# The second half of x of pair 1, issued behind the constant table and the first mask of pair 0

## The chip, the cores and the metric

The kernel runs on one core of one Trainium2 chip. The metric is the device time of one execution in microseconds. Before the change it is 122.68 us, the median of three runs (122.57 to 123.12). The engines are named as in the profile: PE is TensorE (PEld its weight load), DVE is VectorE, ACT is ScalarE, POOL is GpSimd, SP is SyncE, which here only issues DMAs.

## The reference

A state-space attention step (Mamba-2 form) is followed by a bilinear feed-forward. Per batch and head the sequence of 768 is worked in chunks, with a decaying state carried from chunk to chunk:

```
M       = (C B^T) * L                       # L: decay between two positions, causal
y       = M x + (C state) * decay_to_i
state   = decay_full * state + sum_j B_j x_j * decay_from_j
out     = ((y Wa) * (y Wb)) Wout            # 3072 tokens, 256 -> 1536 -> 256
```

There are 4 batches, 8 heads, head size 32 and state size 16; x, B, C and the weights are float32 in memory, and the kernel computes its products in float16.

## The kernel before, in words

The 768 positions are cut into 6 blocks of 128 (the decay is arranged so that a block of 128 replaces the reference's chunks of 32). The 4 batches are taken two at a time, so that there are 12 "pairs": pair p is block p // 2 of batches 2(p % 2) and 2(p % 2) + 1. Pairs 0 and 1 are the first block of all batches.

For each pair the kernel scales B and C by decay factors (scale_bc), transposes them on PE (transposes), multiplies them into scores (scores, L458 for the first pairs), masks these with the causal table (mask, L497 on DVE or L494 and L495 on ACT and POOL), scales x to float16 (scale_x, L366 on ACT), and multiplies masked scores by x (pv, whose matmuls are L518). The result is evacuated to X2T (for pair 1 by ACT in L581) and is the moving operand of the feed-forward: matmuls with Wa and Wb (L734 in units_mm, L721 in unit_mm), a copy of the Wa part (L745, ACT), a product (L752, DVE) and the output matmuls with Wo.

The order of the work is written out by hand: the tile framework runs under a manual schedule, every engine executes its instructions in the order of the program, and tile dependencies become semaphore waits. A dependency that the data do not ask for can be added with tc.add_manual_dep. One stands here already: the first half of x of pair 1 waits for f0, the first reciprocal on DVE (L874, L875).

A pair's x is 256 KB in float32. For the first four pairs it is loaded in two halves, one for each of the two batches (load1, whose DMA is L165 for all callers). For pair 1 both halves are issued on SP's queue in L246 and L247, ahead of the constant table c32 (L248, 32 x 148 float32, read by POOL in L942 and by PE in L963). At the same time POOL issues the loads of B and C of pair 1 and then the first halves of the weights (L259 to L263): Wa in two pieces, then Wb in two pieces, with a cast to float16 on the way. The second halves of the weights follow on POOL in L897 and L898. SP's next DMA after these is the store of the decay rows, in L958.

The first work on both weights is that of pair 0: three groups of Wa matmuls for pair 0 (L915, L918, L919), with the scores and masks of pair 1 between them, and three groups of Wb matmuls (L931, L933 to L935), with pv(1), the product of pair 1's masked scores and its x, standing behind the first four of them (L932). On ACT the order there is: the copy of the first Wa group (L920), scale_x(1) in L921, the copies of the second and third group (L922), and then the evacuation of pv(1). So x of pair 1 is wanted by ACT between the first and the second copy.

The four masks of pair 0 are DVE's L889, L890, L894 and L895, each a product of 128 x 512 scores with the causal table. The first of these is the one that the change names.

Of the kernel before, what the change touches and what calls it, by code (L numbers as in the profile page):

```python
# [14 lines left out]
ALU = mybir.AluOpType  # L15
PSUM = bass.MemoryType.PSUM
AFTER = mybir.DependencyInfo(mybir.DependencyClass.Sync, mybir.DependencyReason.DATA)
# [12 lines left out]
def kernel(  # L30
# [13 lines left out]
    nc = tc.nc  # L44
# [109 lines left out]
    def by_token(t_):  # L154
        return t_.rearrange("p h r n -> p (h r n)").rearrange("p (t h n) -> p t h n", t=2, h=H)

    def load1(eng, p, which, bt, i0=0, n=64):
        blk, bp = divmod(p, NBP)
        if p >= P0:
            return eng.dma_start(  # L160
                by_token(pair_in[p][which])[:, bt],
                (B, C, x)[which][2 * bp + bt, :, blk * Q : (blk + 1) * Q, :].rearrange("h q n -> q h n"),
            )
        src = (B, C, x)[which][2 * bp + bt, :, blk * Q + 2 * i0 : blk * Q + 2 * i0 + 2 * n, :]
        return eng.dma_start(  # L165
            pair_in[p][which][64 * bt + i0 : 64 * bt + i0 + n].rearrange("i h r n -> i h (r n)"),
            src.rearrange("h (i r) n -> i h (r n)", r=2),
        )
# [57 lines left out]
    for p_ in range(3):  # L226
# [17 lines left out]
    nc.vector.memset(c32, 0.0)  # L244
    nc.vector.memset(Pq, 0.0)
    x1 = load1(nc.sync, 1, 2, 0)  # L246
    load1(nc.sync, 1, 2, 1)  # L247
    nc.sync.dma_start(c32[0:BH], p32_t.ap())  # L248
    nc.gpsimd.affine_select(
        out=ident, in_=ident, compare_op=ALU.is_equal, fill=0.0, base=0, pattern=[[-1, 128]], channel_multiplier=1  # L250
    )
    for bt in range(2):
        v = causal[64 * bt : 64 * bt + 64]
        nc.gpsimd.affine_select(  # L254
            out=v, in_=v, compare_op=ALU.is_ge, fill=0.0, base=0, pattern=[[-1, 2], [1, Q]], channel_multiplier=-2
# [46 lines left out]
    def second_factors(fps):  # L302
        F = fps[:, 0:32].rearrange("p (r c) -> p r c", r=2)
        for r in range(2):
            for bt in range(2):
                nc.tensor.matmul(
                    F[64 * bt : 64 * bt + 64, r],
                    Pr[:, 1].rearrange("p (i r) -> p r i", r=2)[:, r],
                    selr[:, bt].rearrange("p b h -> p (b h)"),
                    start=True,  # L310
                    stop=True,
                    skip_group_check=True,
                    tile_position=(0, 64 * bt),
                )
# [167 lines left out]
    def product0(m2, e):  # L482

        return (
            st[0]["T1"][:, 4 * m2 : 4 * m2 + 4].rearrange("p (m e) r q -> p e m (r q)", e=2)[:, e],
            (SC0, SC1)[m2][:, :, e * 256 : e * 256 + 256],
            causal.rearrange("p r q -> p (r q)").unsqueeze(1).broadcast_to((128, 2, 2 * Q)),
        )

    def mask(out_in, by_pool=False):  # L490
        o_, i_, c_ = out_in
        if by_pool:
            tmp = mid.tile([128, *c_.shape[1:]], f32, name="tmp", tag="tmp")
            nc.scalar.copy(tmp, i_)  # L494
            nc.gpsimd.tensor_tensor(out=o_, in0=tmp, in1=c_, op=ALU.mult)  # L495
        else:
            nc.vector.tensor_tensor(out=o_, in0=i_, in1=c_, op=ALU.mult)  # L497

    def pv_u(p, u, py, first, flip=2):
        s = st[p]  # L500
# [365 lines left out]
    def pull(p):  # L866
# [19 lines left out]
    scores(0)  # L886
    fps = bank("fps")
    second_factors(fps)
    mask(product0(0, 0))  # L889
    mask(product0(0, 1))  # L890
    scale_bc(1, 0, nc.gpsimd)
    scale_x(0, nc.scalar)
    nc.scalar.copy(f_c(1), fps[:, 0:32].rearrange("p (r b h) -> p r b h", r=2, b=NBP))
    mask(product0(1, 0))  # L894
    mask(product0(1, 1))  # L895
    scale_bc(1, 1, nc.gpsimd)
# [3 lines left out]
        out=causal_q, in_=causal_q, compare_op=ALU.is_ge, fill=0.0, base=0, pattern=[[1, Q]], channel_multiplier=-1  # L900
# [25 lines left out]
    for w in range(2):  # L926
# [16 lines left out]
        out=hsx[0:BH],  # L943
        in0=hs.unsqueeze(1).broadcast_to((BH, nb, NG)),
        in1=selb.rearrange("p (b g) -> p b g", b=nb),
        op=ALU.mult,
# [291 lines left out]
```

## Time and profile before

| | us |
|---|---|
| median of three runs | 122.68 |
| the profiled execution | 122.38 |
| its span, first to last instruction | 120.6 |
| PE busy | 116.2 (96%) |
| DVE busy | 93.0 (77%) |
| ACT busy | 75.4 (62%) |
| POOL busy | 70.3 (58%) |

The granted TensorE clock is 1.0 throughout. The profile's times are counted from the start of the span. "Busy" leaves out DMA-issuing instructions and waits. A DMA issue is shown on the queue of the engine that issues it (SPq, ACTq, POOLq), and its "landing" is counted from the start of that issue to the completion. The DMA queues are q1 (issued by SP), q10 (issued by ACT) and q0 (issued by POOL); all of them share 16 DMA engines. The chain is followed back from the last instruction to whatever released each step.

### The profile page before, as it was taken

To read this page: it belongs to the slowest core of one execution; us is meant where nothing else is said; L and a number is where in the kernel's file an instruction comes from. 1 tells how busy PE (TensorE), PEld (TensorE's weight loads), DVE (VectorE), ACT (ScalarE), POOL (GpSimd) and SP (SyncE) were. 2 spreads that over 40 slices of the span, in tenths; PEclk is the share of its full clock that TensorE was granted. 3 is DMA by queue.
4 is the path that set the end of the run, shared out by engine and by line. 5 is a ranking of instruction groups with operands and counts; after the bars stand their busy time and mean duration, and the time that the engine had idled before them with its cause. 6 is when DMAs were issued, how large, how long until landed. Compare 5 with 4: busy or idle time off the path is not lost.

```text
span 120.6 us, 3714 instructions
## 1 busy us (share of the span) xinstructions
PE 116.2 (96%) x1436; PEld 79.2 (66%) x1436; DVE 93.0 (77%) x184; ACT 75.4 (62%) x155; POOL 70.3 (58%) x96
## 2 busy tenths in 40 slices
PE   6999999999999999999999999999999999999990
PEld 2346789889898898644476464686464684555890
DVE  4999999994998979699995999767998445847100
ACT  0458867837668856987669657655866737566220
POOL 7995999999996997199998099119043000000000
PEclk9999999999999999999999999999999999999999
DMA  3999989993886593866469701012001012010122
GB/s 64 194 167 213 211 179 224 152 192 66 91 160 118 51 137 75 133 87 150 108 191 232 242 8 43 0 49 87 3 0 43 7 42 87 0 43 5 43 87 87
DMA packets 35953, 12.29 MB, mean 102 GB/s; under 512 B 29840, under 2 KB 35248, under 8 KB 35936
## 3 DMA queue, kind: packets, MB, share of 16 engines
q1 hardware_dynamic: 30976, 6.71, 27.3%
q0 software_dynamic: 2688, 4.92, 20.1%
q10 hardware_dynamic: 2272, 0.43, 1.8%
q8 instruction: 11, 0.18, 0.6%
q14 instruction: 6, 0.05, 0.2%
HBM read 11.20 MB, written 3.21 MB: 119 GB/s over the span
## 4 chain that ended last, share of the span: by engine, by line
PE 87%; DMA 5%; POOL 4%; issue 1%; ACT 0%; DVE 0%
PE ops L824 18%; PE aps L799 17%; PE bps L799 17%; PE ops L767 9%; PE aps L721 8%; PE bps L721 8%; DMA Wb<-in_moe_w_b_dram 5%; PE SC L443 2%; PE SC L503 1%; PE bps L734 1%; POOL bn L165 1%; POOL cn L165 1%; PE SC L518 1%; PE tr L409 1%; POOL causal L254 1%
## 5 line engine op out<-in xcount | busy, mean ns | idle before, releaser
L745 ACT COPY asb<-aps 128x512 f32<-128x512 f32 x71 | 41.3, 587 | 12.8 <-PE aps L799 8.8
L809 DVE TENSOR_TENSOR hkb<-bps,asb 128x512 f16<-128x512 f32 x48 | 32.1, 690 | 10.2 <-ACT asb L745 9.7
L799 PE MATMUL aps<-XB,Wa 128*128 128x512 f16 x96 | 28.6, 379 | 0.0
L799 PE MATMUL bps<-XB,Wb 128*128 128x512 f16 x96 | 28.5, 379 | 0.0
L824 PE MATMUL ops<-Wo,hkb 128*128 128x256 f16 (+1 forms) x204 | 22.6, 266 | 0.0
L824 PEld LDWEIGHTS <-hkb 128*128 128x128 f16 x204 | 18.6, 98 | 3.1
L497 DVE TENSOR_TENSOR t<-SC,causal_q 128x512 f16<-128x512 f32 x24 | 15.5, 683 | 2.4 <-PE SC L443 2.4
L799 PEld LDWEIGHTS <-Wb 128*128 128x128 f16 x96 | 9.9, 103 | 10.9
L752 DVE TENSOR_TENSOR hk<-bps,asb 128x512 f16<-128x512 f32 x24 | 15.8, 685 | 1.5 <-ACT asb L745 1.3
L495 POOL TENSOR_TENSOR t<-tmp,causal_q 128x512 f16<-128x512 f32 x8 | 9.2, 1160 | 13.0 <-ACT tmp L494 12.7
L799 PEld LDWEIGHTS <-Wa 128*128 128x128 f16 x96 | 9.7, 103 | 9.2
L836 ACT ACTIVATE osb<-ops 128x256 f32<-128x256 f32 (+1 forms) x16 | 6.1, 378 | 12.3 <-PE ops L824 12.2
L721 PE MATMUL bps<-X2T,Wb 128*128 128x256 f16 x84 | 12.4, 272 | 0.0
L368 POOL TENSOR_SCALAR x<-xn 128x512 f16<-128x512 f32 x8 | 11.9, 1489 | 0.7
L721 PE MATMUL aps<-X2T,Wa 128*128 128x256 f16 x80 | 11.9, 273 | 0.0
L767 PE MATMUL ops<-Wo,hk 128*128 128x256 f16 x96 | 11.6, 273 | 0.0
L767 PEld LDWEIGHTS <-hk 128*128 128x128 f16 x96 | 8.9, 98 | 1.3
L721 PEld LDWEIGHTS <-Wa 128*128 128x128 f16 x84 | 8.4, 104 | 0.8 <-issue 0.2
L721 PEld LDWEIGHTS <-Wb 128*128 128x128 f16 x84 | 8.6, 103 | 0.5
L497 DVE TENSOR_TENSOR t<-SC,causal 128x512 f16<-128x512 f32 x13 | 8.2, 681 | 0.4 <-PE SC L458 0.3
L494 ACT COPY tmp<-SC 128x512 f32<-128x512 f32 x11 | 6.5, 592 | 1.7 <-PE SC L458 0.6
L202 DVE STREAM_TRANSPOSE tq<-mq 128x256 f16<-128x256 f16 x10 | 7.5, 745 | 0.0
(115 smaller groups left out, 142.1 us busy)
## 6 DMA issues: line engine op xcount, KB each, us to landing
out_dram<-osb SPq DMA_DIRECT2D x18, 128.0 KB, 2.1
xn<-in_x_dram POOLq DMA_DIRECT2D x6, 256.0 KB, 5.2
rq<-in_C_dram SPq DMA_DIRECT2D x32, 32.0 KB, 3.0
Wo<-in_moe_w_out_dram POOLq DMA_DIRECT2D x2, 384.0 KB, 5.8
bn<-in_B_dram SPq DMA_DIRECT2D x6, 128.0 KB, 4.6
out_dram<-osb SPq DMA_DIRECT2D x11, 64.0 KB, 1.5
xn<-in_x_dram SPq DMA_DIRECT2D x4, 128.0 KB, 5.2
xn<-in_x_dram SPq DMA_DIRECT2D x2, 256.0 KB, 5.3
```

Source lines behind the costliest of these rows:

```text
L202: nc.vector.transpose(t_.rearrange("p t (i g) -> p g t i", g=4), st[("scaled", blk, which)][:, :, 2 * bp : 2 * bp + 2].rearrange("p g t e ...
L368: eng.tensor_scalar(xo, xi, XS, None, ALU.mult)
L494: nc.scalar.copy(tmp, i_)
L495: nc.gpsimd.tensor_tensor(out=o_, in0=tmp, in1=c_, op=ALU.mult)
L497: nc.vector.tensor_tensor(out=o_, in0=i_, in1=c_, op=ALU.mult)
L721: nc.tensor.matmul(ps[:, kk * 2 * Q : (kk + 1) * 2 * Q], w_up(W, k, f), X2T[:, p, :, f], start=(f == 0), stop=(f == 1), skip_group_check=True,
L745: (nc.vector.tensor_copy if on_dve else nc.scalar.copy)(asb, a_ps)
L752: nc.vector.tensor_tensor(out=s["hk"][:, 2 * k2 : 2 * k2 + 2, :].rearrange("p k q -> p (k q)"), in0=b_ps, in1=asb, op=ALU.mult)
L767: nc.tensor.matmul(o_ps[:, 0:d_model], hk[:, k, bt * Q : (bt + 1) * Q], Wo[:, k, :], start=(k == 0), stop=(k == NK - 1), skip_group_check= ...
L799: nc.tensor.matmul(t_, w_up(W, k, f), XB[:, blk - P0 // NBP, f].rearrange("p t j q -> p (t j q)"), start=(f == 0), stop=(f == 1), skip_gro ...
L809: return lambda: nc.vector.tensor_tensor(out=s["hk"][:, k], in0=ps[1], in1=asb, op=ALU.mult)
L824: nc.tensor.matmul(o_ps[:, 0:w], hk[:, k, c * Q : (c + 1) * Q], Wo[:, k, cs], start=(k == 0), stop=(k == NK - 1), skip_group_check=True,)
```

## The change

The second half of x of pair 1 is issued behind the constant table on SP's queue. It also gets a manual dependency on the first mask of pair 0, so that SP waits for that DVE instruction before it issues the load. For this, mask() returns the DVE instruction.

```diff
     x1 = load1(nc.sync, 1, 2, 0)
-    load1(nc.sync, 1, 2, 1)
     nc.sync.dma_start(c32[0:BH], p32_t.ap())
+    x1b = load1(nc.sync, 1, 2, 1)
...
         else:
-            nc.vector.tensor_tensor(out=o_, in0=i_, in1=c_, op=ALU.mult)
+            return nc.vector.tensor_tensor(out=o_, in0=i_, in1=c_, op=ALU.mult)
...
     scores(0)
     fps = bank("fps")
     second_factors(fps)
-    mask(product0(0, 0))
+    m0 = mask(product0(0, 0))
+    tc.add_manual_dep(x1b.ins, m0.ins.name, AFTER, reason="weights ahead of the second half of pair 1's x")
     mask(product0(0, 1))
```

## The prediction

> **What bounds the kernel now.** I read the chain that ended last first, over the first 15 us, where the moved load and everything it feeds lie (columns: start, length in us, what).
>
> ```profile
> 6.23 6.09 DMA Wb<-in_moe_w_b_dram
> 12.32 0.05 issue
> 12.37 0.62 PE bps L734 x4
> 12.99 0.40 PE SC L518 x32
> 13.39 0.99 PE bps L734 x8
> ```
>
> The chain runs through a weight transfer, Wb, up to 12.37, and from there on TensorE (PE) alone. The reader is to see two things: the weight is what PE waited for here, and 0.6 us later PE does the L518 matmuls, which multiply by x of pair 1. So I asked next how much idle time PE has, before and after this place (windows of time; the columns are the stretch, its length, busy us of PE, PEld, DVE, ACT, POOL, the granted clock, the DMA share and GB/s).
>
> ```profile
> 5.70:14.40 8.70, 8.07 (x177) 5.06 (x177) 8.14 (x21) 6.38 (x17) 7.23 (x13) 1.00 1.13 199
> 14.40:117.90 103.50, 103.41 (x1250) 72.69 (x1249) 80.94 (x148) 67.50 (x138) 58.22 (x72) 1.00 0.45 93
> ```
>
> From 14.4 to 117.9 PE is idle for 103.50 - 103.41 = 0.09 us. Work that PE starts late at 14.4 therefore ends late by the same amount: there is nothing behind it that could take a delay up. Between 5.7 and 14.4 it is idle for 8.70 - 8.07 = 0.63 us. That is all that better-timed loads could win here.
>
> Third, the timeline of ScalarE (ACT) at that place. It shows who makes the x that L518 needs.
>
> ```profile
> 11.76 0.58 ACT L745 COPY asb<-aps 128x512 f32<-128x512 f32 x1
> 12.24 0.63 ACT L366 ACTIVATE x<-xn 128x512 f16<-128x512 f32 x1
> 12.78 1.06 ACT L745 COPY asb<-aps 128x512 f32<-128x512 f32 x2
> 13.72 0.62 ACT L581 ACTIVATE X2T<-SC 128x512 f16<-128x512 f32 x1
> ```
>
> ACT has no gap from 11.76 to 14.34. The scaling of x of pair 1 (L366) starts at 12.24 because the copy ahead of it is done, with no wait on a load listed. Behind it in order stand two copies and the evacuation into X2T, whose end at 14.34 releases PE's L721 matmuls at 14.39. A late L366 thus delays L518 and, through ACT's order, L721 by the same time.
>
> Fourth, when the halves of x arrive: the tile xn between 5 and 14 us.
>
> ```profile
> L165 SPq DMA_DIRECT2D xn<-in_x_dram x2: 601/618/636, 5.2 to 5.9; - x2
> DMA to landing us min/median/max: 5.1/5.6/6.0
> ```
>
> The first half, issued at 5.2, takes 5.1 us (lands 10.3); the second, issued at 5.9, takes 6.0 (lands 11.9). ACT needs it at 12.24, so the half that is moved has 0.35 us to spare.
>
> **The change, part by part.**
>
> The handle that mask() now returns issues no instruction: 0.
>
> The constant table takes the second half's place on SyncE's queue, at 5.9 instead of 6.54, and its 0.62 us issue then ends at 6.5. It took 5.6 us and landed at 12.1; its first reader is POOL at 16.97 (L942). Earlier is worth 0, and even 4.8 us later would cost nothing. On SP's queue the load waits now, and behind it stands only the store of rows at 17.82, which waits 10.6 us for DVE; a load issued by 8.8 is 9 us clear of it. POOL's queue is not touched: 0.
>
> The wait on the first mask is the main part. DVE runs four masks from 7.43, in order:
>
> ```profile
> 4.94 0.25 DVE L874 RECIPROCAL fB<-fC 128x16 f32<-128x16 f32 x1
> 7.43 2.48 DVE L497 TENSOR_TENSOR t<-SC,causal 128x512 f16<-128x512 f32 x4
> ```
>
> One takes 0.68 (median by line), so the first ends at 8.11. The first half hangs in the same way on L874, which ends at 5.19, and is issued at 5.2, so a release costs some 0.03 to 0.05. The second half is issued at 8.15, that is 2.25 us later than now. With 0.35 to spare this is late by 1.9 us if it still takes 6.0, and harmless if it takes 4.1 or less. On DVE the extra signal can cost at most some 0.02 (one semaphore event of that line is 21 ns), which the 2.48 us row of masks absorbs or passes on once; I take 0.
>
> How long does it take from 8.15? The bounds: 4.2 us, the one 128 KB half that ACT's queue issued at 2.9, before any weight was asked for, and 6.0, the moved half itself, which now queues right behind the first half. The four x loads of this size on SP took 5.1, 6.0, 5.3 and 5.1. I take 5.1, the first half of the same x: same size and queue, weights moving beside it, and no other half right ahead, which is what the moved half will meet. Packets by window bear this out (queue, packets, MB, share of 16 engines; the three fences are 7 to 8 us, 8 to 9 us and 11 to 12 us):
>
> ```profile
> q0 software_dynamic: 83, 0.12, 89.4%
> q1 hardware_dynamic: 11, 0.00, 1.9%
> ```
>
> ```profile
> q0 software_dynamic: 85, 0.11, 63.6%
> q1 hardware_dynamic: 465, 0.12, 53.9%
> ```
>
> ```profile
> q0 software_dynamic: 140, 0.19, 107.6%
> q1 hardware_dynamic: 33, 0.01, 9.3%
> ```
>
> SP's queue (q1) moves almost nothing from 7 to 8 though the first half's issue ended at 5.85: its bytes start some 2.1 us after that, and last from 8.0 to 10.3, its landing. The weights (q0) keep the engines as busy at 11 as at 7, so a half issued at 8.15 to 8.77 starts at about 10.9 and lands at 10.9 + 2.3 = 13.2, which agrees with 8.15 + 5.1 = 13.25.
>
> The sum: L366 starts 0.04 after landing (pair 0's last piece landed at 7.39 and its L366 began at 7.43), at 13.29 instead of 12.24: +1.05 us. All that follows on ACT and PE shifts by that. With the bounds, 4.2 gives 12.39, so +0.15; 6.0 gives 14.19, so +1.95.
>
> Against it stands what the weights gain. The moved half's bytes ran mostly between 9 and 11 us; q1 held 54, 38 and 36% of the engines from 8 to 11, some 1.3 us for both halves, so 0.6 for one. Wb, then without that company, can land up to 0.6 us earlier, and PE's 0.21 us wait before 12.37 goes. It is worth nothing: the four L734 matmuls finish 0.21 earlier and PE then stands before L518, waiting for L366. That wait is late next, with x undelayed until 12.87, with the change until 13.92. I book 0, with 0.2 as its bound.
>
> The profiled execution took 122.38 (span 120.6 and 1.8 around it), 0.30 under the median of 122.68. 122.38 + 1.05 = 123.43 on its own scale, 123.73 on the median's. I predict 123.7.
>
> **The rivals.**
>
> Hidden (not slower). The half starts moving soon after its issue and lands before 12.2, so nobody waits. For it: the very first load on this queue, issued from 0.80 to 1.20, moves its first packets before 2.0, at most 0.8 us after the issue. With that start the half would begin at 8.77 + 0.8 = 9.6 and land at 9.6 + 2.3 = 11.9, and the time would be 122.7, at best 122.5 with the 0.2 of Wb. Against it: that load met idle engines, the first half met weights and needed 2.1. It decides at a flight of 4.1 us; up to 4.65 the loss stays under 0.6. The Trainium skill (DMA: Bandwidth & Descriptors, Specifications) gives about 0.6 us to the first byte on this path, which speaks for this rival: by it the landing would be some 11.7 and the sum 0; the trace agrees for the first load and not for the first half of x. Chance 0.23, counting every loss below 0.6.
>
> Later still. The half shares the engines with four more weight transfers (two of 192 KB under way, two of 384 KB issued at 8.63 and 9.38) and again takes 6.0: +1.95, 124.6. For it: q0's share is above 100% from 11 us on. Against it: three of four such loads took 5.1 to 5.3. Chance 0.14, for anything over 5.8 us.
>
> Faster. Wb lands early, x lands in time as well, and all of PE's 0.63 us of idle time before 14.4 goes: 122.05. That idle time has other owners (only 0.21 is put down to Wb). Chance 0.03.
>
> **How the numbers follow.** The forecast, a flight of 4.65 to 5.8 us, has 0.60 and its own range of 123.3 to 124.4. About 0.5%, 0.6 us, is what a measurement of this kernel can tell from no change. Slower is forecast plus later still, 0.74; within it 0.23; faster 0.03. The range of 122.6 to 124.6 leaves out the faster case (0.03), some 0.07 of the hidden one and 0.09 of the late one.
>
> **What would show it.** In the changed kernel's profile: the second half's issue at 8.1 to 8.2, with the table's before it at 5.9; a flight near 5.1 us; ACT idle between the first L745 copy (ending 12.34) and L366 for about 1 us, released by the load of xn; PE idle about 1 us before L518, with the first four L734 starting at 12.2; L721 at about 15.4; Wb no longer in the chain, xn in its place. It is wrong if L366 still starts at 12.24 (the hidden case), if the flight is far from 5.1, or if PE's stall does not show at the end, which would mean idle time behind 14.4 that the windows do not show.

## The result, and the profile after

The changed kernel takes 124.36 us in the median of six executions, against 122.75 of the kernel before beside it: 1.6 us slower, a ratio of 1.014 (95% interval 1.010 to 1.018). A second measurement of the same kernel gave 1.009 (1.006 to 1.012). In some executions of the kernels that stall here the granted clock is 0.973 to 0.987 and the time one to some five us longer; the medians keep these, the ratios leave them out where they are over 1.5% above the fastest, and one of 125.47 us stays in the 1.014, which would be 1.012 without it.

The profiled execution took 124.28, with a span of 122.6 instead of 120.6. The chain that ended last, from 7 to 18 us (start, length in us, what):

```profile
7.40 0.72 DVE t L497 x2
8.12 5.97 DMA xn<-in_x_dram
...
14.71 1.05 ACT asb L745 x2
15.77 0.51 ACT X2T L581
16.27 0.04 issue
16.32 0.60 PE aps L721 x4
```

It now runs through the first mask, then through the moved half of x in place of Wb, and then through ACT's order, up to the L721 matmuls. These start at 16.32 instead of 14.39, 1.93 us later, and the span grew by 2.0. ACT's timeline at that place (start, length, what; in brackets the idle time before it and what ended it):

```profile
11.87 0.58 ACT L745 COPY asb<-aps 128x512 f32<-128x512 f32 x1 [0.22 <-PE aps L734]
14.18 0.63 ACT L366 ACTIVATE x<-xn 128x512 f16<-128x512 f32 x1 [1.73 <-DMA xn<-in_x_dram]
14.71 1.05 ACT L745 COPY asb<-aps 128x512 f32<-128x512 f32 x2
15.65 0.61 ACT L581 ACTIVATE X2T<-SC 128x512 f16<-128x512 f32 x1
```

ACT waits 1.73 us for the load before L366, and everything behind keeps its distance: 14.18 to 15.65 is 1.47, and was 12.24 to 13.72. PE's timeline:

```profile
12.70 0.62 PE L734 MATMUL bps<-X2T,Wb 128*128 128x256 f16 x4 [0.43 <-DMA Wb<-in_moe_w_b_dram]
14.86 0.42 PE L518 MATMUL SC<-t,x 64*32 64x128 f16 x32 [1.54 <-ACT x L366]
15.21 1.05 PE L734 MATMUL bps<-X2T,Wb 128*128 128x256 f16 x8
```

Wb was not even earlier in this execution, but 0.33 us later (12.70 after 12.37). Behind the stall PE is as full as it was (window of time; stretch, length, busy us of PE, PEld, DVE, ACT, POOL, clock, DMA share, GB/s):

```profile
16.30:119.90 103.60, 103.42 (x1250) 72.69 (x1249) 80.86 (x148) 67.61 (x138) 56.64 (x70) 1.00 0.44 90
```

It is idle for 0.18 us in 103.6, so none of the delay is taken back.

The tile xn, from 8 to 15 us: the moved half alone.

```profile
L165 SPq DMA_DIRECT2D xn<-in_x_dram x1: 601/601/601, 8.1 to 8.1; - x1
DMA to landing us min/median/max: 6.0/6.0/6.0
```

The issue is at 8.12 and the flight 6.0, where the prediction took 5.1. In the repeat the half was issued at 8.20 and flew 5.3:

```profile
13.59 0.63 ACT L366 ACTIVATE x<-xn 128x512 f16<-128x512 f32 x1 [1.19 <-DMA xn<-in_x_dram]
```

L721 starts there at 15.73, against 14.60 in a profile of the kernel before on the same chip: +1.13 for a wait of 1.19. The two profiles of the change differ as the two flights do; that the two ratios differ for this reason alone was not shown.

### The profile page after: what moved, and what is told of

The parts are those of the page before. It is cut to its first block, busy times and chain, and to the rows that moved or that the text cites. A ratio compares the mean times of both kernels' runs of the same rounds, so it can differ in the third digit from the quotient of the medians.

```text
span 122.6 us, 3715 instructions
## 1 busy us (share of the span) xinstructions
PE 115.7 (94%) x1436; PEld 78.9 (64%) x1436; DVE 93.1 (76%) x184; ACT 75.5 (62%) x155; POOL 70.7 (58%) x96
## 4 chain that ended last, share of the span: by engine, by line
PE 85%; DMA 7%; DVE 3%; ACT 2%; issue 1%; DVEq 0%; ACTq 0%
PE ops L824 17%; PE aps L799 17%; PE bps L799 17%; PE ops L767 9%; PE aps L721 8%; PE bps L721 7%; DMA xn<-in_x_dram 5%; PE SC L443 2%; DMA a_sb<-in_a_dram 2%; PE SC L503 1%; PE SC L458 1%; ACT asb L745 1%; DVE fC L289 1%; PE tr L409 1%; ACT bt L413 1%
## 5 line engine op out<-in xcount | busy, mean ns | idle before, releaser
L824 PEld LDWEIGHTS <-hkb 128*128 128x128 f16 x204 | 18.6, 98 | 3.1
L799 PEld LDWEIGHTS <-Wb 128*128 128x128 f16 x96 | 9.9, 103 | 10.9
L836 ACT ACTIVATE osb<-ops 128x256 f32<-128x256 f32 (+1 forms) x16 | 6.0, 378 | 12.3 <-PE ops L824 12.2
L721 PE MATMUL bps<-X2T,Wb 128*128 128x256 f16 x84 | 12.4, 272 | 0.0
L368 POOL TENSOR_SCALAR x<-xn 128x512 f16<-128x512 f32 x8 | 11.9, 1489 | 0.7
L721 PE MATMUL aps<-X2T,Wa 128*128 128x256 f16 x80 | 11.9, 273 | 0.1
L721 PEld LDWEIGHTS <-Wa 128*128 128x128 f16 x84 | 8.4, 105 | 0.9 <-issue 0.2
L721 PEld LDWEIGHTS <-Wb 128*128 128x128 f16 x84 | 8.6, 103 | 0.5
```

The lines of the kernel that those rows point to most:

```text
L368: eng.tensor_scalar(xo, xi, XS, None, ALU.mult)
L721: nc.tensor.matmul(ps[:, kk * 2 * Q : (kk + 1) * 2 * Q], w_up(W, k, f), X2T[:, p, :, f], start=(f == 0), stop=(f == 1), skip_group_check=True,
L799: nc.tensor.matmul(t_, w_up(W, k, f), XB[:, blk - P0 // NBP, f].rearrange("p t j q -> p (t j q)"), start=(f == 0), stop=(f == 1), skip_gro ...
L824: nc.tensor.matmul(o_ps[:, 0:w], hk[:, k, c * Q : (c + 1) * Q], Wo[:, k, cs], start=(k == 0), stop=(k == NK - 1), skip_group_check=True,)
```

## The experiments

Two questions were open. Which part of the change costs the time, the order on SP's queue or the wait? And is the flight a constant, so that a us of later issue is a us of loss once the 0.35 us to spare is used up? The theory at the start, "lateness", said yes to the second; the rivals were the order and contention with the weights. Diffs are against the kernel that is named.

**Only the order changed** (against the changed kernel):

```diff
-    tc.add_manual_dep(x1b.ins, m0.ins.name, AFTER, reason="weights ahead of the second half of pair 1's x")
```

> Theory (lateness): only the landing of the second half of x of pair 1 against ACT's need at 12.24 us counts. Here the table goes first and the half follows without a wait, issued at 6.5 instead of 5.9; with a flight of 5.1 to 6.0 us it lands at 11.6 to 12.5, so 0 to 0.3 us is lost: ratio 1.000 to 1.003. Rival (order): the loss comes from giving up the place ahead of the table on SP's queue; then most of the 1.6 us shows here, ratio about 1.013.

Measured: 123.80, ratio 1.010 (1.007 to 1.013). This is a miss for the lateness theory. The half is issued 0.7 us later than before, at 6.55, and nothing waits for a mask, yet most of the loss is there:

```profile
13.68 0.63 ACT L366 ACTIVATE x<-xn 128x512 f16<-128x512 f32 x1 [1.14 <-DMA xn<-in_x_dram]
```

The flight is 7.0 us. ACT's wait, 1.14, accounts for the 1.2 us; what was wrong is when the half lands.

**Only the wait** (against the changed kernel):

```diff
-    nc.sync.dma_start(c32[0:BH], p32_t.ap())
     x1b = load1(nc.sync, 1, 2, 1)
+    nc.sync.dma_start(c32[0:BH], p32_t.ap())
```

> The half keeps its place ahead of the table but waits for the first mask; the table then waits behind it. Theory (lateness): the half is issued at 8.1 and lands at 13.3 to 14.2 as in the changed kernel, the loss is the same 1.1 to 2.0 us, ratio 1.009 to 1.016; the table, issued at 8.7 and landed by 15, has no reader before 17 and costs nothing. Rival (order): no loss, ratio 1.000.

Measured: ratio 1.017 (1.010 to 1.024) from three executions. The half is issued at 8.16, flies 5.5 and lands at 13.7; ACT waits 1.38 in the profiled execution (123.88). The table, issued at 8.81, is waited for by nobody. So either part alone costs about as much as both (1.010 and 1.017, beside 1.014 and 1.009). They do not add up, and the rival, order, would have left no loss here.

**The wait on an earlier instruction** (against the changed kernel; the reciprocal L282 in place of the mask):

```diff
-    over_mid(1, 2)
+    r1 = over_mid(1, 2)
+    tc.add_manual_dep(x1b.ins, r1.ins.name, AFTER, reason="second half of pair 1's x behind the second block's factors")
...
-    tc.add_manual_dep(x1b.ins, m0.ins.name, AFTER, reason="weights ahead of the second half of pair 1's x")
```

> The changed kernel with the wait on an earlier DVE instruction, the reciprocal that ends at 6.85 us, instead of the first mask (8.1). Theory (lateness): issue at 6.9, 1.2 us earlier than in the changed kernel, landing at 12.0 to 12.9, loss 0 to 0.7 us, ratio 1.000 to 1.006, and ACT's wait before the scaling about 1.2 us shorter than in the changed kernel (1.73). Rival (contention: what costs is that the half now travels beside the Wb transfers and delays these): loss about as in the changed kernel, since Wb is still under way when the half lands, ratio about 1.012, with PE's wait on Wb grown instead.

Measured: 123.83 and 123.73 in two executions at a clock of 1.0, beside 122.59, that is 1.01; the other two, at 0.986 and 0.973, took 128.04 and 128.67, and there is no interval. Issue at 6.97, 1.15 us earlier than in the changed kernel, and the half lands at 13.6 all the same:

```profile
13.71 0.63 ACT L366 ACTIVATE x<-xn 128x512 f16<-128x512 f32 x1 [1.25 <-DMA xn<-in_x_dram]
```

PE did not wait for Wb here. Both theories missed: the loss did not shrink with the earlier issue, and though the rival had its size right, Wb was not the one that paid.

**The wait on the last mask** (against the changed kernel):

```diff
-    m0 = mask(product0(0, 0))
+    mask(product0(0, 0))
...
-    mask(product0(1, 1))
+    m3 = mask(product0(1, 1))
+    tc.add_manual_dep(x1b.ins, m3.ins.name, AFTER, reason="second half of pair 1's x behind pair 0's last mask")
```

> The changed kernel with the wait on the last of pair 0's masks, which ends at 9.9 us, 1.8 later than the first. Theory (lateness): issue at 9.95, landing at 15.0 to 16.0, loss 2.8 to 3.8 us, ratio 1.023 to 1.031: each us of later issue is a us of loss. Rival (contention): the loss does not grow with the delay, ratio about 1.014.

Measured: 130.13, ratio 1.062 (1.055 to 1.070), twice the expected loss. The half is issued at 9.97 and flies 8.6 us, to 18.6:

```profile
18.64 0.63 ACT L366 ACTIVATE x<-xn 128x512 f16<-128x512 f32 x1 [6.26 <-DMA xn<-in_x_dram]
```

So the landing goes in steps: 11.9 to 12.3 for issues at 5.9, 13.5 to 14.1 for issues from 6.55 to 8.2, 18.6 for 9.97. A second theory was formed: the half's bytes stand behind whatever weight pieces POOL has issued ahead of it. POOL issues Wa's two pieces at 5.1 to 6.3, Wb's two at 6.2 to 7.4, and in the last kernel the two 384 KB second halves at 9.04 and 9.79, both ahead of the half.

**No weights beside it** (against the changed kernel; Wb's first half is zeros, so the output is that of zero weights there, and the second halves are issued later):

```diff
-    load_w(Wb, 0, 0)
-    load_w(Wb, 0, 1)
+    nc.gpsimd.memset(Wb[0].bitcast(u32), 0)
...
-    load_w(Wa, 1)
-    load_w(Wb, 1)
...
+    load_w(Wa, 1)
+    load_w(Wb, 1)
     tiles(3)
```

> The changed kernel without most of the weight transfers beside the half: the first half of Wb is filled with zeros on POOL instead of being loaded (the output is that of zero weights there), and the second halves of Wa and Wb are issued after pair 2's inputs, some 5 us later. The time says nothing; the flight of the second half of x is looked at. Theory (weights set the flight): about 4.0 us, landing by 12.3, ACT's wait gone. Rival (the flight is the path's own): 5.1 to 6.0 again.

Measured: a flight of 3.5 us from the same issue time, and no wait on ACT. Tile xn from 8 to 15 us:

```profile
L165 SPq DMA_DIRECT2D xn<-in_x_dram x1: 602/602/602, 8.2 to 8.2; - x1
DMA to landing us min/median/max: 3.5/3.5/3.5
```

**Only the second halves later** (against the changed kernel; as above, with Wb's first half left where it was):

```diff
-    load_w(Wa, 1)
-    load_w(Wb, 1)
...
+    load_w(Wa, 1)
+    load_w(Wb, 1)
     tiles(3)
```

> The changed kernel with the second halves of Wa and Wb (384 KB each) issued after pair 2's inputs instead of at 9.2 and 10.0; Wb's first half stays where it is. The flight of the moved half is looked at, not the time, which the late second halves spoil. Theory (the pieces of Wb ahead of it set the flight): 5.3 to 6.2 us as in the changed kernel. Rival (the 384 KB pieces behind it set the flight): about 3.5 to 4.5 us, as in the kernel that had neither.

Measured: a flight of 5.7 us. So Wb's two pieces of 192 KB, issued ahead of the half, set its flight, and the 384 KB behind it do not. The DMA queues in the windows 9.5 to 11.5 and then 11.5 to 12.5 us (packets, MB, share of 16 engines; the times of all packets are added up, so that a share can exceed 100%), first for this kernel:

```profile
q0 software_dynamic: 270, 0.37, 106.6%
q1 hardware_dynamic: 80, 0.02, 6.2%
...
q0 software_dynamic: 69, 0.08, 48.1%
q1 hardware_dynamic: 405, 0.10, 46.1%
```

then for the changed kernel:

```profile
q0 software_dynamic: 275, 0.38, 108.3%
q1 hardware_dynamic: 103, 0.03, 8.5%
...
q0 software_dynamic: 105, 0.14, 80.9%
q1 hardware_dynamic: 347, 0.09, 39.8%
```

and for the first of the two windows only, the kernel before, and then the one without Wb:

```profile
q0 software_dynamic: 214, 0.29, 86.6%
q1 hardware_dynamic: 532, 0.14, 35.4%
```

```profile
q1 hardware_dynamic: 602, 0.15, 35.0%
q0 software_dynamic: 62, 0.07, 20.8%
```

In the changed kernel the half's issue is over at 8.72, but SP's queue (q1) moves almost nothing until 11.5, while the weights (q0) fill the engines. Then it moves 347 packets in a us. Before the change, and without Wb, these packets run from about 9.5 on.

**The table first** (against the kernel before):

```diff
+    nc.sync.dma_start(c32[0:BH], p32_t.ap())
     x1 = load1(nc.sync, 1, 2, 0)
     load1(nc.sync, 1, 2, 1)
-    nc.sync.dma_start(c32[0:BH], p32_t.ap())
```

> The kernel before with the table ahead of both halves, in the time in which SP waits for f0 anyway; the halves are issued at 5.2 and 5.9 as before. Theory (moment of issue): the second half goes out ahead of the Wb pieces, which POOL issues from 6.25 on, its bytes start near 9.5 and it lands at 11.9 to 12.3; ratio 1.000, ACT without a wait before L366. Rival (order on SP's queue: a table ahead of the half is what slowed it in the kernel where only the order was changed): landing near 13.6, ACT's wait near 1.1 us, ratio about 1.010.

Measured: ratio 1.001 (0.996 to 1.005), the half issued at 5.9 and landed at 12.0, ACT without a wait:

```profile
12.26 0.63 ACT L366 ACTIVATE x<-xn 128x512 f16<-128x512 f32 x1
```

A table ahead of the half costs nothing as long as the half still goes out at 5.9. What the order alone cost is then put down to the 0.62 us by which the table's issue held the half back; the next run delays it by as much without the table.

**A small delay, the order kept** (against the kernel before):

```diff
-    load1(nc.sync, 1, 2, 1)
+    x1b = load1(nc.sync, 1, 2, 1)
...
-    scan(1, 2)
+    s1 = scan(1, 2)
+    tc.add_manual_dep(x1b.ins, s1.ins.name, AFTER, reason="second half of pair 1's x behind the second block's scan")
```

> The kernel before, order kept, but the second half waits for the scan that ends at 6.3 us, so it is issued at 6.35 instead of 5.9, with the table behind it. Theory (moment of issue): 0.5 us of delay puts its issue beside Wb's first piece and its bytes behind more weights: landing after 13, ACT's wait about 1 us, ratio about 1.009. Rival (order): nothing but 0.5 us of delay, landing 12.4 to 12.8, ACT's wait 0 to 0.5, ratio 1.000 to 1.004.

Measured: 123.86, ratio 1.008 (1.004 to 1.011). In the profiled execution, the fastest of the set (123.15), the half was issued at 6.46, flew 6.5 and landed at 13.0:

```profile
13.04 0.63 ACT L367 ACTIVATE x<-xn 128x512 f16<-128x512 f32 x1 [0.55 <-DMA xn<-in_x_dram]
```

The interval agrees with the moment of issue, and excludes no loss; the profiled wait of 0.55 lies just above what the rival gave (0 to 0.5) and below the theory's 1. Some 0.6 us of later issue cost 0.9 us.

**Wb later** (against the kernel with only the order changed):

```diff
+    nc.gpsimd.memset(Wo[:, 0:6].bitcast(u32), 0)
     load_w(Wb, 0, 0)
```

> The kernel where only the order was changed (table ahead, half issued at 6.55, no wait), with 0.74 us of other POOL work (a fill with zeros, of a tile that is loaded later) ahead of Wb's first piece, which is then issued at 7.0. Theory (the half's place relative to the Wb pieces counts): the half is again ahead of Wb, its bytes start near 9.5 to 10 and land near 12.2, ACT's wait before L366 goes from 1.14 to 0.3 at most; the loss is then Wb's own 0.7 us at most. Rival (the clock time of the issue counts, whatever POOL issues): bytes near 11.5, landing 13.6, ACT's wait 1.1 as before.

Measured: 1.011 (1.001 to 1.020) from two executions, and ACT's wait before the scaling unchanged at 1.14, landing at 13.8. The half went out at 6.75 in this execution and Wb at 7.01, so the two issues, 0.6 and 0.5 us long, overlap. The bytes did start earlier: q1 moved 429 packets from 9.5 to 11.5, against 196 with only the order changed. But its last ones came as late as before. The theory of the place ahead of Wb is met in its first half and missed in its second, so what exactly an SP load has to be ahead of stays open.

**Extra PE work in the stall** (against the changed kernel):

```diff
+    warmup(5, SC[3][:, 256:512], 2)
     pv(1)
```

> The changed kernel with five extra 256-column warm-up matmuls on PE (some 0.22 us each, 1.1 us) ahead of the product with x of pair 1, in the time in which PE waits; their result is not used. Theory (lateness): PE only waits there, so 1.1 us of added work costs nothing, ratio 1.009 to 1.017 as the changed kernel. If idle PE is what lowers the granted clock in some executions, these show 1.0 throughout and the median falls by up to 0.2 us. Rival (PE is bound in this stretch): +1.1 us more, ratio about 1.023.

Measured: ratio 1.011 (1.007 to 1.014), beside 1.009 for the changed kernel on the same chip. The five matmuls took 0.71 us, not 1.1, and cost nothing measurable: PE still waited 0.83 us for L366 behind them. The half, issued at 8.33, landed at 14.6 in this profile. The granted clock was 0.986 in two of six executions all the same (and 0.997 in a third, which the kernel before shows too), so the fill did not end it.

**Both kernels once more**, for their flight times:

> The kernel before, once more, for its flight times on the chip that the next runs share. Theory (flight varies): the first half of x, whose place is the same in both kernels, took 5.1 us in one profile of the kernel before and 6.4 in that of the changed one; if this is variation from run to run, it lies anywhere from 5.1 to 6.4 here. Rival (the change slows it): 5.1 again.

> The changed kernel once more. Theory (lateness): ratio 1.009 to 1.017, with ACT's wait before the scaling of x of pair 1 equal to the growth of the span within 0.2 us. If the flight varies from run to run, the second half's is 5.1 to 6.4 us and the loss follows it. The granted clock fell to 0.986 in two of six earlier executions; theory (idle PE): some executions again below 1.0.

Measured: the kernel before 122.59 (ratio 1.000), the first half's flight 6.2 and the second's 6.5, where the first profile had 5.1 and 6.0. Its second half landed at 12.3 and ACT, whose own order had come to 12.43, did not wait. The changed kernel: ratio 1.009, and flights of 5.6 and 5.3. The first half, which nothing in the change touches, thus varies from 5.1 to 6.4 between these four profiles, and from 4.4 to 6.4 over all fourteen; this is variation, not an effect of the change.

No kernel here beats the one before; the one with the table first equals it.

## Why the prediction was right

The sign, the place and the range held: 124.36 lies within 122.6 to 124.6, and the mechanism is that of the forecast. Its size, +1.05, was met by the repeat (1.009, or 1.1 us) and was too small for the first measurement (+1.6). That the size came this near is in part luck, since the flight behind it was reasoned wrongly.

- *What the change does at SP.* The issue at 8.15 was 8.12, the table's at 5.9 was 5.83, and SP's store came at 19.88, still clear of the moved load. The table at 0: right, in every order tried.
- *ACT and PE shift by the lateness.* Right in the three profiles compared: waits of 1.73, 1.19 and 6.26 us on ACT (the change, its repeat, the wait on the last mask) answer to later starts of L366 of 1.94, 1.16 and 6.2 us, the first against 12.24 in the first profile of before, the others against 12.43 in its repeat. No idle time behind took anything back.
- *The weights' gain at 0.* Right, though not as told. In the first profile Wb was later, and its wait grew from 0.21 to 0.43. In the repeat the wait is gone (L734 at 12.05, against 12.79 in the repeat of before), and the time is no better for it, since PE then waits for L366.
- *The flight of 5.1.* This is the term that was mis-sized: 6.0 and 5.3 were measured. By its flight the first profile is the rival "later still" (6.0, L366 later by 1.94 where it said 1.95), and the second is the forecast. The step took a duration from one row of one profile, and that row itself varies by 2.0 us from run to run (4.4 to 6.4). That 10.9 + 2.3 agreed with 8.15 + 5.1 was no second source: both sums move the same issue, start and landing of the first half by the same amount.
- *"With 0.35 to spare ... harmless if it takes 4.1 or less".* The reasoning that the flight is the load's own and the moment of issue merely shifts it was wrong, although it did little harm to the number. An issue 0.7 us later already cost 1.2 us, and a further 1.6 us of delay cost next to nothing. The flight depends on the weight pieces in the load's way: 3.5 us without Wb, 5.3 to 7.0 with it, 8.6 with the two 384 KB pieces issued ahead too. The prediction's window rows showed the first half starting 2.1 us after its issue; they were read as a fixed start, not as a queue. The true start for the moved half was 2.8 us after the end of its issue (8.72 to 11.5).
- *The hidden rival.* It lost because of Wb, not because the path is slow. Without Wb on the way the bytes start at about 9.5, some 0.8 us after the end of the issue (8.76), as the first load's did, and ACT's wait is gone. The Trainium skill (DMA: Bandwidth & Descriptors, Specifications) gives about 0.6 us to the first byte: the run without Wb comes near it, and the changed kernel, with 2.8, does not.

## What to carry to other kernels

A load's flight read from one profile belongs to the moment of its issue, not to the load: here 0.6 us of later issue cost 0.9 us, and beyond 0.7 us a further 1.6 us cost next to nothing. So ask which transfers will stand ahead of it and when these land, not only how long the load took: in the first profile of before Wb's second piece lands at 13.2, and the moved half then landed 0.4 to 0.5 us behind that piece. Before a load is moved for the sake of others, find who needs those others: here the weights that were to gain fed matmuls which had to stop for the moved load anyway.

## What the runs showed of the hardware

The steps of the landing were not expected: 11.9, 13.0, 13.6, 13.6, 14.1, 13.5, 14.6 and 18.6 us for issues at 5.86, 6.46, 6.55, 6.97, 8.12, 8.20, 8.33 and 9.97. They go with the landings of the weights. In the seven profiles where the half went out between 6.55 and 8.33 and Wb's issues were where they are in the kernel before, it landed 0.3 to 0.5 us behind Wb's second piece, wherever that one fell between 13.0 and 14.1; with the wait on the last mask it landed 0.5 us behind the second 384 KB piece (18.05). Where it went out at 5.8 to 6.5 (both profiles of before, the table first, the small delay) it landed 0.3 to 0.6 us ahead of the Wb piece that was issued next. Order of issue alone does not give this: with only the order changed the half went out 0.2 us before Wb's second piece, and with Wb later 0.8 us before it, and it still landed behind.

On engines that the weights keep busy (q0 at 108%), the changed kernel's load on SP's queue got almost no share for 2.8 us and then ran at some 350 packets per us; with the wait on the last mask this took over 3 us, and it ran at 235 at most. What ends the waiting, the weight queue running low or something in the engines, was not settled.

A long stall has a price beyond its length. In the kernel that waits for the last mask PE is idle for 6.5 us; its windows from 12 to 45 us (the granted clock is the third number from the right):

```profile
12.00:19.00 7.00, 0.79 (x6) 0.34 (x4) 2.06 (x6) 0.74 (x2) 6.79 (x12) 0.71 1.10 207
19.00:24.00 5.00, 4.68 (x52) 3.34 (x53) 2.40 (x4) 2.60 (x6) 1.61 (x3) 0.50 0.82 159
24.00:45.00 21.00, 21.00 (x365) 18.36 (x364) 17.52 (x36) 13.15 (x27) 14.91 (x20) 0.97 0.54 95
```

After the stall PE runs at half its clock for about 6 us, from 19.3 to 25.2; four L721 matmuls take 1.06 us there and 0.60 otherwise. Its span is 8.7 us above that of the repeat of before (129.6 and 120.9) while L366 starts 6.2 us later, so by this estimate some 2.5 us are the clock's. The Trainium skill (TensorE: Matmul & The Clock Gate, Part 1) says that the clock halves after an idle window of about 3.4 us. The trace shows the halving, but after a shorter time: PE's last matmul ends at 12.81, the clock is 0.96 in the mean from 14.5 to 15 and 0.50 from 15 on, so it fell at about 14.96, some 2.2 us into the stall.

Waits of two us were enough in another run. With only the second halves later, PE waits 2.10 us for the late Wa, works for 1.3 us and waits 1.90 us for Wb; the clock is 1.00 from 21 to 22, 0.58 from 22 to 23, and 0.50 from there to 29. In stalls of 1.5 us the profiles keep 1.0, but other executions of the same kernels show 0.973 to 0.987, with one to some five us more, while 51 executions of the kernel before show none below 0.997; that the shorter stall causes it is likely by this, but no trace of such an execution shows it.
